# Two orders for one kernel: the task list of all engines, the places of its tiles and the engines of its PSUM copies are drawn up anew

## The chip, the cores and the metric

The kernel runs on one core of one Trainium2 chip. The core has five engines that each work through their own queue in order: TensorE (PE in the profile, with its weight loads as PEld), VectorE (DVE), ScalarE (ACT), GpSimd (POOL) and SyncE (SP). SP and POOL issue the transfers here. The metric is device time in microseconds of one launch.

## The reference

Two independent heads are computed and set side by side in the output. Head A shifts k by a filter of four taps, multiplies with v, convolves each channel over the whole sequence with a long filter (through a Fourier transform), adds a skip term and multiplies with q. Head B is a state space model: a complex projection of x, a recurrence over time with one complex factor for each state, a projection back, and a skip term.

```python
# head A, S = 2048, D = 1024
kv = k_shift * v
y_f = rfft(pad(kv)) * rfft(pad(ssm_k))
a = q * (irfft(y_f)[:S] + kv * ssm_D)
# head B, L = 2048, 1024 states
Bu = einsum("bld,pd->blp", x, B_bar)
h = Lam_bar * h + Bu[:, t, :]          # for each t
b = 2.0 * einsum("blp,dp->bld", hseq, Cmat).real + x * Dskip
return concatenate([a, b], axis=-1)
```

## The kernel before

The whole program is a list of 1489 words, the string `ORDER` (lines 68 to 188). A word such as `U.5.3.0:a22p5` names a task, its indices, and the places of new tiles: `a` is a unit of the SBUF arena (53 units of 1024 columns), `p` one of the eight PSUM banks, `h` one of three slots for the state g, `w` one of three slots for Fourier weights. A loop (lines 767 to 781) calls the tasks in the order of the list. Each engine works off its own tasks in the order of the list; between engines only data and reused places make anything wait.

Head B works in 16 chunks of 128 time steps. `x.i` loads a chunk transposed (L449, on SP). `U.i.jp.jl` is a sixteen-matmul piece of the projection on the whole 128x128 array (L468); two pieces share a bank and `ue.i.jp` copies it to SBUF on ScalarE, or `uev` on VectorE (L473). On VectorE follow `r1` and `r2` (rotation, L486 and L493), two scans `sc` (L499) and `r3`, `r4` (L486, L505); `cy` carries the last state over on ScalarE (L495). The projection back is `y` on the whole array (L515, L518) for chunks 0 to 2, 14 and 15, and `yq` for chunks 3 to 13: eight steps of 20 matmuls that use four 64x64 quarters of the array at once (L533). `ye` copies the result (L551) and `yst`, `ysp`, `ysh`, `ysg` store it.

Head A forms kv on VectorE (`kvm`, `kva`, `kvb`, `kvc`), transforms it on the whole array (`am`, L602, copied by `ae`) and stores it to HBM (`ast`). The filter goes through `hT` (whole array), `hm` (quarters, L651) and `he`. The second stage works on 16 pairs i: `lw.i` loads the weights into a slot (L666, on SP), `lh.i` and `lk.i` load rows (L671), `sh` and `sk` transform them on quarters (L682), `she` and `ske` copy the results (L691, L698), `sw` (POOL) or `swp` (SP) swap halves of one of them by a transfer (L702), `pr` multiplies on VectorE (L708), `sa` transforms back on quarters (L720), `sae` copies and `vst` stores. The last stage is `vl` (load), `a3` (whole array, L748), `a3e`, `qm` (product with q) and the store `ost` or `osp`.

At the start, `bl`, `bT`, `bc` load, transpose and copy the matrix B (whole array), and `cl`, `cT`, `cc`, `cx` the matrix C; `wb` and `wbe` spread the four filter taps over the partitions.

A name with a v at its end (`shev`, `a3ev`, `bcv`, `hdv` and so on) is the same copy on VectorE instead of ScalarE.

Of the kernel before, what the change touches and what calls it, by code (L numbers as in the profile page):

```python
# [29 lines left out]
GW = 130  # L30
# [37 lines left out]
bl.5.1:a45 bT.5.1:p6 ld_par par_T:p1 bc.5.1 bl.2.0:a25 ld_F ld_w:a26 wb.0:p0 kp.0:a0 p32 wb.2:p4 wbe.0:a8 dd wb.5:p5  # L68
bl.7.0:a32 wbe.2 bl.0.1:a34 exp1 wb.4:p3 dve2 bl.5.0:a33 dve3 bT.2.0:p6 wb.6:p2 wbe.5 bl.4.0:a49 sm_pre wbe.4
bl.4.1:a17 exp2 wb.3:p7 bl.1.1:a47 bc.2.0 wb.7:p6 wbe.3 sin0 kp.1 bT.0.1:p0 bT.7.0:p4 wbe.7 wbe.6 bl.6.1:a16 bT.4.0:p1  # L70
bc.0.1 bc.7.0 bl.0.0:a46 tabA1:a24a51a14a12 kp.-1 bT.1.1:p2 x.0:a47 par_rest cl.0.0:a39 wb.1:p7 bT.5.0:p5 sin1
bl.3.0:a31 bcv.4.0 bT.0.0:p3 wbe.1 bT.4.1:p6 bc.1.1 tabA2 kring bl.3.1:a46 kvm.3:a26 gz bT.6.1:p1 bc.0.0 bl.1.0:a23
bc.4.1 U.0.2.0:a34p4 U.0.0.0:p2 sin2 bc.6.1 bl.2.1:a22 bT.3.1:p0 bc.5.0 x.1:a33 eo kvm.2:a18 kvm.1:a40 U.0.2.1
bT.1.0:p5 kva.2 cT.0.0:p1 bT.2.1:p3 bc.2.1 bT.3.0:p6 kva.1 kvb.2:a38 kva.3 bc.3.0 U.1.2.0:a36p7 stt U.1.2.1 bl.6.0:a50
bT.6.0:p3 kvb.1:a46 bl.7.1:a32 bc.3.1 U.0.1.0:p6 bT.7.1:p0 kp.-2 bc.1.0 bc.6.0 bc.7.1 U.0.1.1 U.0.0.1 ue.0.0 ue.0.1
vp.1:a48 cl.2.0:a22 z2 z1 cl.1.1:a31 cc.0.0 x.3:a21 cl.2.1:a44 ue.1.2 ue.0.2 U.0.3.0:p3 U.0.3.1 kvb.3:a32 ue.0.3
U.1.3.0:p6 U.1.0.0:p2 kvm.0:a13 cT.2.0:p0 U.1.3.1 U.1.1.0:p5 kvc.3 kvc.2 kva.0 r1.0:a48 cc.2.0 lw.1:w0 cl.1.0:a30
ue.1.3 cx.5.1 U.1.0.1 ue.1.0 cT.1.0:p3 cc.1.0 cl.3.0:a45 kvb.0:a39 am.2.1:p4p0 ae.2.1.1:a28 rta r2.0:h0 am.2.0:p6p2
cT.2.1:p1 cc.2.1 U.1.1.1 ue.1.1 cT.3.0:p3 vp.0:a42 kvc.1 U.3.2.0:a34p7 cc.3.0 ae.2.0.1 kvc.0 ae.2.0.0 kp.3 sc.0.1
U.3.2.1 hl.0.1:a24 cl.3.1:a20 cT.3.1:p0 sc.0.0 cc.3.1 am.3.0:p5p1 ae.3.1.0:a22 ae.2.1.0 r1.1:a42 hl.0.0 U.3.3.0:p3  # L80
U.3.3.1 cT.1.1:p0 cc.1.1 kp.2 hl.1.0:a48 cl.0.1:a38 ue.3.2 am.3.1:p4p1 ae.3.1.1 U.3.0.0:p6 ue.3.3 U.3.0.1 ue.3.0
ae.3.0.0 hl.1.1 am.1.1:p0p2 ae.1.1.1:a30 cx.5.0 am.0.0:p1p7 ae.0.1.0:a18 ae.3.0.1 r3.0:a12 hdv.1 ast.2 hdv.0 ast.3
# [12 lines left out]
hm.0.1.0:p0p6 he.0.1.1.1:a38 he.0.1.0.1 y.1.0.2 vp.2:a28 hst.0.4.0 he.0.1.0.0 y.1.0.3 kvc.4 r2.2:h0 cy.2 he.0.0.0.0
ye.1.0:a18 kvc.5 am.5.1:p5p6 am.5.0:p4p2 am.4.1:p0p1 y.1.1.0:p3 y.1.1.1 he.0.1.1.0 hst.0.0.0 ae.5.1.1:a36 ae.4.0.1:a28
ae.5.1.0 hst.0.0.1 kp.5 am.4.0:p7p6 y.1.1.2 ae.4.1.0 vp.3:a26 ae.5.0.1 y.1.1.3 hl.3.0:a40 ae.5.0.0 hl.3.1 hd.3
ae.4.0.0 kvm.7:a12 hst.0.1.0 hl.2.0:a44 sc.2.1 kvc.6 hl.2.1 hd.2 am.6.0:p4p2 kva.7 ae.6.0.0:a22 ae.4.1.1 ast.5 sc.2.0
U.4.3.0:p6 ye.1.1 ae.6.1.0 kvb.7:a19 U.4.3.1 r3.2:a48 ue.4.3 am.6.1:p0p5 hT.1.1:p4 ae.6.0.1 kp.4 hc.1.1:a33 hT.1.3:p3
hc.1.3:a16 hst.0.1.1 ae.6.1.1 U.4.2.0:p2 hT.1.7:p0 U.4.2.1 yst.1 hc.1.7:a20 ue.4.2 ast.4 hT.1.6:p7 hc.1.6:a38  # L100
kvm.8:a12 U.4.0.0:p4 kvc.7 U.4.0.1 ue.4.0 r4.2 hT.1.0:p6 kva.8 ast.6 hc.1.0:a39 am.7.1:p0p2 am.7.0:p7p1 ae.7.1.0:a28
hT.1.4:p3 yst.0 hst.0.7.0 hc.1.4:a18 hst.0.2.0 ae.7.1.1 kvm.9:a48 y.2.0.0:p4 x.6:a37 ae.7.0.0 hm.1.3.1:p5p6 kvb.8:a36
he.1.3.1.1:a26 y.2.0.1 he.1.3.1.0 y.2.0.2 ae.7.0.1 cy.3 hm.1.7.1:p7p1 hm.1.3.0:p6p5 he.1.7.1.0:a16 hm.1.7.0:p3p0
he.1.3.0.1 he.1.3.0.0 he.1.7.0.1 he.1.7.0.0 kva.9 y.2.0.3 ye.2.0:a19 sc.3.1 vp.4:a22 y.2.1.0:p7 hT.1.2:p2 sc.3.0
hm.1.4.1:p0p6 hm.1.4.0:p3p5 kvc.8 hT.1.5:p4 r3.3:a44 y.2.1.1 ast.7 kvb.9:a18 y.2.1.2 hst.0.7.1 hst.1.3.1 he.1.7.1.1
y.2.1.3 he.1.4.1.0:a12 he.1.4.1.1 hst.1.3.0 hc.1.5:a20 he.1.4.0.1 he.1.4.0.0 am.8.1:p5p6 r4.3 ye.2.1 hst.1.4.1
# [84 lines left out]
def full_kernel(ctx, tc, A_q, A_k, A_v, A_shift_k, A_ssm_k, A_ssm_D, B_x, B_Lre, B_Lim, B_Bre, B_Bim,  # L191
# [645 lines left out]
```

## Time and profile before

| what | value |
|---|---|
| time, median of 3 runs | 349.76 us (347.51, 349.76, 351.59) |
| span of the profiled execution, first to last instruction | 346.5 us |
| the profiled execution's own time | not listed apart from the three |
| granted TensorE clock | 0.998 of full speed |
| TensorE busy | 328.0 us, weight loads 237.5 us |
| VectorE busy | 325.2 us |
| ScalarE busy | 272.3 us |
| GpSimd busy | 69.3 us |

Times in the profile are microseconds from the span's start. A row of groups gives line, engine, operation, tiles, count, then busy time and mean length of one in ns, then the idle time of that engine just before, with what ended it. Matmuls overlap in TensorE's pipeline and their ends are modelled, so starts are the safer reading.

### The profile page before, as it was taken

The numbers are of one execution on the slowest core, as the hardware profiler recorded it, in microseconds if no ns is written. First come the engines' busy times: TensorE is split into PE (matmuls) and PEld (weight loads), VectorE is DVE, ScalarE is ACT, GpSimd is POOL, SyncE is SP. The second block draws the span as 40 slices with busy tenths as digits, with TensorE's granted clock in tenths as the row PEclk, the third lists the DMA queues.
The fourth block names the chain that finished last, engine by engine and source line by source line (L and its number), as shares of the span: only waits on it lengthen the run. The fifth ranks groups of instructions, "written<-read, shape, count | busy, mean of one in ns | idle before, by whom it ended". The sixth has DMA issues, their size and how long they took to land.

```text
span 346.5 us, 11774 instructions
## 1 busy us (share of the span) xinstructions
PE 328.0 (95%) x5086; PEld 237.5 (69%) x5105; DVE 325.2 (94%) x263; ACT 272.3 (79%) x520; POOL 69.3 (20%) x114
## 2 busy tenths in 40 slices
PE   5889899999999999999999999999699999999994
PEld 2678789654856777688957877775376789754442
DVE  3999799999999999999999999999799999999991
ACT  6999999998999884599668899899689893314741
POOL 5000002142343163121100222211021133000021
PEclk9999999999999999999999999999999999999999
DMA  6999999979979879997896689999998898998995
GB/s 214 340 292 261 354 271 275 254 264 307 334 248 248 281 245 301 281 241 277 303 343 205 226 313 344 262 353 330 276 289 297 312 334 287 295 391 270 340 405 205
DMA packets 62752, 101.09 MB, mean 292 GB/s; under 512 B 29422, under 2 KB 31742, under 8 KB 62700
## 3 DMA queue, kind: packets, MB, share of 16 engines
q1 hardware_dynamic: 52652, 65.81, 63.7%
q0 software_dynamic: 10048, 34.52, 27.8%
q8 instruction: 40, 0.66, 0.8%
q14 instruction: 12, 0.10, 0.1%
HBM read 52.08 MB, written 33.55 MB: 247 GB/s over the span
## 4 chain that ended last, share of the span: by engine, by line
PE 68%; ACT 17%; DVE 7%; DMA 4%; issue 2%; SPq 1%; DVEq 0%; ACTq 0%
PE bank L468 24%; PE bank L533 15%; PE bank L515 10%; PE bank L682 4%; PE bank L720 4%; ACT BT L433 4%; PE bank L748 3%; PE bank L602 3%; DVE gslot L499 3%; PE bank L651 2%; ACT arena L608 2%; DMA wslot<-a_c_W 2%; ACT CT L441 2%; DVE arena L486 2%; ACT arena L473 2%
## 5 line engine op out<-in xcount | busy, mean ns | idle before, releaser
L468 PEld LDWEIGHTS <-BT 128*128 128x128 bf16 x2048 | 116.2, 98 | 13.0 <-issue 8.2
L468 PE MATMUL bank<-arena,BT 128*128 128x128 bf16 x2048 | 122.6, 219 | 1.6 <-DMA arena<-in_B_x_dram 0.9
L533 PE MATMUL bank<-CT,gslot 64*64 64x512 bf16 x1408 | 87.6, 377 | 0.0
L499 DVE TENSOR_TENSOR_SCAN gslot<-rtab,gslot 128x1040 bf16<-128x1040 f32 x32 | 73.0, 2312 | 0.1
L533 PEld LDWEIGHTS <-gslot 64*64 64x64 bf16 x1408 | 43.4, 107 | 23.9 <-ACT arena L698 0.6
L473 ACT CAST arena<-bank 128x512 bf16<-128x512 f32 x63 | 38.8, 655 | 11.6 <-PE bank L468 11.6
L608 ACT CAST arena<-bank 128x512 bf16<-128x512 f32 x64 | 37.2, 670 | 5.8 <-PE bank L602 4.9
L515 PE MATMUL bank<-CT,gslot 128*128 128x512 bf16 x154 | 38.1, 380 | 0.6 <-issue 0.3
L691 ACT CAST arena<-bank 128x512 bf16<-128x512 f32 x59 | 32.5, 615 | 7.8 <-PE bank L682 7.2
L486 DVE TENSOR_TENSOR arena<-arena,Z 128x4096 bf16<-128x4096 bf16 x16 | 36.5, 2284 | 2.2 <-ACT arena L473 2.1
L708 DVE TENSOR_TENSOR arena<-arena 128x4096 bf16<-128x4096 bf16 x16 | 36.3, 2285 | 1.7 <-ACT gslot L495 0.8
L728 ACT CAST arena<-bank 128x512 bf16<-128x512 f32 x61 | 33.3, 630 | 5.4 <-PE bank L720 5.3
L486 DVE TENSOR_TENSOR arena<-gslot,Z 128x4096 bf16<-128x4096 bf16 x16 | 36.6, 2288 | 0.3
L698 ACT CAST arena<-bank 128x512 bf16<-128x512 f32 x61 | 34.2, 616 | 3.3 <-PE bank L682 2.8
L659 ACT CAST arena<-bank 128x512 bf16<-128x512 f32 x64 | 35.2, 689 | 1.0 <-PE bank L651 0.7
L551 ACT CAST arena<-bank 128x512 bf16<-128x512 f32 x29 | 17.7, 616 | 16.3 <-PE bank L533 8.7
L582 DVE TENSOR_TENSOR arena<-arena 128x4096 bf16<-128x4096 bf16 (+3 forms) x16 | 30.0, 1886 | 0.1
L662 POOL DMA_DIRECT2D Ys_h<-arena x32 | 22.9, 728 | 29.0 <-ACT arena L659 23.1
L611 POOL DMA_DIRECT2D Ys_kv<-arena x16 | 10.9, 688 | 87.1 <-ACT arena L608 71.8
L515 PEld LDWEIGHTS <-gslot 128*128 128x128 bf16 x160 | 14.0, 98 | 17.1 <-issue 2.6
L702 POOL DMA_DIRECT2D arena<-arena x20 | 10.7, 538 | 70.8 <-ACT arena L691 46.9
L682 PE MATMUL bank<-arena,wslot 64*64 64x512 bf16 x256 | 21.5, 381 | 3.0 <-DMA wslot<-a_c_W 3.0
(104 smaller groups left out, 427.7 us busy)
## 6 DMA issues: line engine op xcount, KB each, us to landing
Ys_kv<-arena POOLq DMA_DIRECT2D x16, 512.0 KB, 4.9
Ys_h<-arena POOLq DMA_DIRECT2D x32, 256.0 KB, 3.8
arena<-Ys_h SPq DMA_DIRECT2D x16, 512.0 KB, 5.3
arena<-Ys_kv SPq DMA_DIRECT2D x16, 512.0 KB, 6.4
Vs<-arena POOLq DMA_DIRECT2D x16, 512.0 KB, 5.8
arena<-Vs SPq DMA_DIRECT2D x16, 512.0 KB, 6.9
arena<-arena POOLq DMA_DIRECT2D x20, 256.0 KB, 4.1
arena<-in_A_k_dram SPq DMA_DIRECT2D x8, 512.0 KB, 6.0
```

Source lines behind the costliest of these rows:

```text
L468: nc.tensor.matmul(pu[:, w, jl, :], BT[:, 2 * jp + jl, w, d, :], xT[:, d, :], start=(d == 0), stop=(d == ND - 1))
L473: either("ue", lambda cp, i, jp: cp(st["u", i][:, :, 2 * jp:2 * jp + 2, :], st.pop(("pu", i, jp))))
L486: nc.vector.tensor_mul(m, s_, win(Z))
L499: nc.vector.tensor_tensor_scan(gf, rtab[:].rearrange("p j t -> p (j t)"), gf, 0.0, ALU.mult, ALU.add)
L515: nc.tensor.matmul(py, h[:, w, j, 2:GW], CT[:, j, w, dh * 512:(dh + 1) * 512], start=(j == 0 and w == 0), stop=False)
L533: mm = nc.tensor.matmul(st["py", i, dh][cols, cs(r)], lhs(dh, rows, c), rhs(dh, rows), start=first, stop=last)
L608: cp(st["ysb", n2][:, p, dh * 512:(dh + 1) * 512], st.pop(("pa", n2, p, dh)))
L659: cp(o, st.pop(("pb", hf, s, e, r)).rearrange("p (n c t) -> p n c t", n=2, c=2))
L682: nc.tensor.matmul(st["ps", nm, g, l][64 * dh:64 * dh + 64, :], st["w", i][rows, a * WC:a * WC + 64], st[nm, i][rows, a, dh * 512:(dh + 1) ...
L698: cp(st["x16", i][:, a, l, :], st.pop(("ps", "k", g, l)))
L708: nc.vector.tensor_mul(hab, st.pop(("x16", i)).rearrange("p a l d -> p (a l d)").unsqueeze(1).to_broadcast([P, 2, 2 * D]), hab)
L728: cp(st["vsb", i][:, a, dh * 512:(dh + 1) * 512], st.pop(("pv", g, dh)))
```

## The change

The list is a new one with the same amount of work. Every engine's order of tasks differs, and so do nearly all places of tiles. On TensorE the same 497 tasks stand in another order; the number of whole-array and quarter tasks is unchanged. A few copies change engine. Counted by task name:

| task | before | after |
|---|---|---|
| `a3e` / `a3ev` | 25 / 7 | 28 / 4 |
| `she` / `shev` | 59 / 5 | 62 / 2 |
| `ske` / `skev` | 61 / 3 | 59 / 5 |
| `sae` / `saev` | 61 / 3 | 60 / 4 |
| `ue` / `uev` | 63 / 1 | 64 / 0 |
| `bc` / `bcv` | 15 / 1 | 14 / 2 |
| `hd` / `hdv` | 2 / 2 | 4 / 0 |
| `sw` (POOL) / `swp` (SP) | 20 / 12 | 15 / 17 |
| `ost` (POOL) / `osp` (SP) | 4 / 4 | 6 / 2 |
| `ysg` (POOL) / `ysh` (SP) | 2 / 2 | 1 / 3 |

Three tasks are also written so that more orders are possible: either half of `U` may come first, the arena places of u are taken at its first copy, and the slot of g is taken by whichever of `cy` and `r2` comes first.

```diff
 ORDER = """
...
-lh.12:a38 sw.10.1 lk.15:a6 vst.4 she.31.1 she.30.1 sw.15.0 sw.15.1 U.12.2.0:p7 sa.22:p2p4 r4.11 sk.21:p3p1 ske.21.1
-swp.10.0 ske.21.0 sa.23:p6p5 ue.12.1 U.12.2.1 U.12.0.0:p1 U.12.0.1 sae.22.1:a20 sae.23.1 sae.23.0 ue.12.2 sk.31:p0p5
...
+she.20.0 she.21.1 sc.11.0 vst.8 U.12.3.1 r3.11:a28 sh.31:p7p4 she.30.0:a2 ue.12.3:a0 U.12.1.1 she.31.0 sa.23:p2p6
+lh.12:a11 she.30.1 she.31.1 ysp.8 swp.10.0 U.12.2.1:p0 sk.20:p5p7 ue.12.1 sa.22:p3p4 yst.10 U.12.2.0 swp.10.1 lw.12:w0
...
     def U(i, jp, jl):
-        if jl == 0:
-            if ("u", i) not in st:
-                st["u", i] = sb(2).rearrange("p (w j t) -> p w j t", w=2, j=NJ)
+        if ("pu", i, jp) not in st:
             st["pu", i, jp] = bank().rearrange("p (w j t) -> p w j t", w=2, j=2)
...
-    either("ue", lambda cp, i, jp: cp(st["u", i][:, :, 2 * jp:2 * jp + 2, :], st.pop(("pu", i, jp))))
+    def ue(cp, i, jp):
+        if ("u", i) not in st:
+            st["u", i] = sb(2).rearrange("p (w j t) -> p w j t", w=2, j=NJ)
+        cp(st["u", i][:, :, 2 * jp:2 * jp + 2, :], st.pop(("pu", i, jp)))
+    either("ue", ue)
...
+    def g_(i):
+        if ("g", i) not in st:
+            st["g", i] = gslots[cur["h"].pop(0)]
+        return st["g", i]
+
     def r2(i):
-        st["g", i] = gslots[cur["h"].pop(0)]
         m = mview(i)
-        nc.vector.tensor_add(st["g", i][:, :, :, 2:GW], m[:, :, 0, :, :], m[:, :, 1, :, :])
+        nc.vector.tensor_add(g_(i)[:, :, :, 2:GW], m[:, :, 0, :, :], m[:, :, 1, :, :])
...
-    E["cy"] = lambda i: nc.scalar.copy(st["g", i][:, :, :, 1], st["g", i - 1][:, ::-1, :, GW - 1])
+    E["cy"] = lambda i: nc.scalar.copy(g_(i)[:, :, :, 1], st["g", i - 1][:, ::-1, :, GW - 1])
```

More of the change, by code (lines that the diff above doesn't have):

```diff
@@ L73 @@
[L73 to L82, printed above, removed]
@@ new lines @@
+sae.23.1:a13 sae.23.0 sk.21:p2p1 r4.11 skev.21.1:a48 U.12.0.0:p6 ske.20.0 U.12.0.1 ue.12.2 sae.22.0 ske.20.1
+yq.11.0:p0p5 ske.21.0 saev.22.1 swp.15.0 ue.12.0 sk.31:p6p7 ske.31.0:a44 pr.10 ske.31.1 sh.25:p2p3 she.25.1:a29
+r1.12:a37 yq.11.1 sh.24:p4p6 she.24.1 she.25.0 yq.11.2 yq.11.3 sk.30:p2p3 she.24.0 ske.30.0 ske.30.1 sa.21:p7p4
+sa.20:p1p6 yq.11.4 sae.21.0:a0 sw.15.1 pr.15 sk.24:p3p2 sae.20.0 yq.11.5 sae.20.1 sk.25:p7p6 lk.14:a19 yq.11.6
+ske.24.1:a48 sa.31:p1p2 vst.7 ske.24.0 sae.21.1 lh.14:a46 sae.31.0:a11 lk.13:a34 skev.25.1 ske.25.0 saev.31.1 sa.30:p3p6
@@ new lines @@
+saev.30.1 yq.11.7 sae.30.0 ye.11.1:a45 cy.12:h2 U.13.3.0:p2 lw.14:w2 swp.12.0 ye.11.0 sh.28:p3p7 lh.13:a24 lw.13:w1
+sk.28:p6p4 she.28.1:a2 sw.12.1 pr.12 sh.29:p1p5 x.15:a44 skev.28.0:a41 U.13.2.1:p0 U.13.2.0 shev.28.0 sh.27:p7p6
+she.29.0 ske.28.1 she.29.1 sk.29:p5p4 r2.12 sh.26:p3p1 she.27.1:a6 U.13.3.1 ysp.9 shev.26.0 swp.14.0 swp.14.1
+U.13.0.1:p6 ske.29.0 she.26.1 vst.10 sk.26:p1p3 she.27.0 sa.25:p5p7 sc.12.1 U.13.0.0 ske.29.1 ske.26.0:a38 sae.25.0:a49
+U.13.1.1:p5 pr.14 sw.13.0 ske.26.1 sk.27:p3p4 ue.13.0:a25 sa.24:p1p6 ue.13.2 ysp.11 sae.24.1 sae.25.1 U.15.3.1:p0
```

215 lines of the change are left out of this document (107 added, 108 removed).

## The prediction

> **What bounds the kernel now.** I read the page first, then the busy time by stage, then the chain of work that ended last, then single stretches of TensorE's timeline. The page:
>
> ```profile
> span 346.5 us, 11774 instructions
> ...
> PE 328.0 (95%) x5086; PEld 237.5 (69%) x5105; DVE 325.2 (94%) x263; ACT 272.3 (79%) x520; POOL 69.3 (20%) x114
> ...
> PE 68%; ACT 17%; DVE 7%; DMA 4%; issue 2%; SPq 1%; DVEq 0%; ACTq 0%
> ```
>
> TensorE and VectorE are both near full, and the chain runs over TensorE for 68% of the span. The busy time of six stages (columns: PE, PEld, DVE, ACT, POOL, clock, DMA share, GB/s), cut where the tasks yq.3.0, yq.5.0, yq.8.0, yq.11.0 and yq.12.0 begin on TensorE, says where each is full:
>
> ```profile
> 0.00:112.20 112.20, 102.55 (x1248) 76.38 (x1261) 104.28 (x118) 106.99 (x188) 26.36 (x47) 1.00 0.96 283
> 112.20:174.00 61.80, 61.48 (x1062) 48.69 (x1067) 61.76 (x46) 46.74 (x94) 16.65 (x25) 1.00 0.89 276
> 174.00:208.90 34.90, 34.18 (x703) 26.13 (x698) 33.98 (x20) 28.67 (x59) 4.32 (x7) 1.00 0.77 265
> 208.90:261.30 52.40, 49.30 (x956) 35.31 (x952) 48.83 (x27) 45.59 (x93) 9.04 (x15) 1.00 1.02 311
> 261.30:298.50 37.20, 37.20 (x684) 29.84 (x679) 35.71 (x26) 26.98 (x56) 8.37 (x13) 1.00 0.90 305
> 298.50:346.50 48.00, 43.30 (x461) 21.19 (x464) 40.69 (x31) 17.33 (x35) 4.56 (x7) 0.98 0.90 322
> ```
>
> In the first stage ScalarE is as full as anything (106.99 of 112.20). From 112 to 298 us TensorE idles 0.32, 0.72, 3.10 and 0.00 us, 4.1 in all. But "busy" on TensorE includes whatever an instruction spends inside the pipeline, so the question is whether it runs at its steady pace. The chain between 150 and 173 us answers it (start, length, what):
>
> ```profile
> 151.30 3.57 PE bank L468 x64
> ...
> 157.53 0.77 PE bank L682 x12
> 158.30 3.75 PE bank L468 x64
> 162.05 0.77 PE bank L682 x12
> 162.82 7.25 PE bank L468 x128
> 170.07 0.77 PE bank L682 x12
> ```
>
> L468 is the projection U, on the whole 128x128 array. Left alone, 64 of its matmuls take 3.57 us, 55.8 ns each. L682 (sh, sk) runs four 64x64 quarters of the array at once. What a quarter matmul of 512 columns costs left alone is seen where quarter work surrounds quarter work:
>
> ```profile
> 211.38 0.86 PE bank L720 x16
> ```
>
> That is 53.8 ns each. So from 157.53 to 162.05 (4.52 us) the steady price of the work is 12 x 53.8 + 64 x 55.8 ns = 4.22 us, and 0.30 us are left over. From 162.05 to 170.07 (8.02 us) it is 0.65 + 7.14 = 7.79, and 0.23 are left over. Nothing waits in either: TensorE alone is on the chain. A third stretch, from quarter work (L533) to the next quarter work:
>
> ```profile
> 135.69 0.84 PE L533 MATMUL bank<-CT,gslot 64*64 64x512 bf16 x12
> ...
> 136.39 1.04 PE L533 MATMUL bank<-CT,gslot 64*64 64x512 bf16 x16
> ...
> 137.29 1.04 PE L533 MATMUL bank<-CT,gslot 64*64 64x512 bf16 x16
> ...
> 139.40 1.07 PE L468 MATMUL bank<-arena,BT 128*128 128x128 bf16 x16
> 140.30 0.38 PE L602 MATMUL bank<-arena,F1t 128*128 128x512 bf16 x1
> 140.74 1.06 PE L468 MATMUL bank<-arena,BT 128*128 128x128 bf16 x16
> 141.63 0.59 PE L602 MATMUL bank<-arena,F1t 128*128 128x512 bf16 x2
> 142.15 0.84 PE L533 MATMUL bank<-CT,gslot 64*64 64x512 bf16 x12
> ```
>
> A yq step takes 0.90 us (136.39 to 137.29) and an am task 0.44 (140.30 to 140.74). Four yq, two U and two am are 3.60 + 1.79 + 0.88 = 6.27 us; the stretch takes 6.46, so some 0.2 us are left over again. Each time TensorE goes from quarter work to whole-array work and back it loses 0.2 to 0.3 us. That loss counts as busy and shows in no wait. From 112 us on TensorE is therefore full in earnest: its work, its switches, and 4.1 us of waits.
>
> **The change part by part.**
>
> *Order on TensorE.* The 497 TensorE tasks are the same. Call T a task on quarters (yq, hm, sh, sk, sa) and F one on the whole array (U, y, am, hT, bT, cT, wb, a3). Counted along the two lists, neighbours of different kind number 64 before and 136 after. By the six stages above: 23, 14, 4, 10, 9, 4 before; 32, 39, 11, 20, 16, 18 after. How it looks in the stretch of U.12 (bars mark the switches):
>
> ```
> before: U.12.3.0 U.12.3.1 | sk.20 sh.30 sh.31 | U.12.1.0 U.12.1.1 U.12.2.0 | sa.22 sk.21 sa.23 | U.12.2.1 U.12.0.0
> after:  U.12.3.0 U.12.1.0 | sh.30 | U.12.3.1 | sh.31 | U.12.1.1 | sa.23 | U.12.2.1 | sk.20 sa.22 | U.12.2.0 | sk.21 | U.12.0.0
> ```
>
> So 36 round trips are added. At 0.2 to 0.3 us each they cost 7 to 11 us; I take 0.26, the mean of the two samples of the chain, whose parts are the purest: **+9.4 us**. By stage: +1.2, +3.3, +0.9, +1.3, +0.9, +1.8. Nothing hides them, because TensorE has only 4.1 us of idle time in the four middle stages; VectorE and ScalarE will wait instead.
>
> [...]
>
> *Engine of the copies out of PSUM.* VectorE loses three a3e, three she and one ue copy and gains two ske and one sae: four fewer. It gains one bc copy and loses two hd additions:
>
> ```profile
> L755 DVE CAST arena<-bank 128x512 bf16<-128x512 f32 x7 | 4.8, 681 | 0.0
> L431 DVE COPY BT<-bank 128x1024 bf16<-128x1024 bf16 x1 | 0.7, 683 | 0.0
> L641 DVE TENSOR_TENSOR arena<-arena,p 128x2 bf16<-128x2 bf16 x2 | 0.2, 161 | 0.0
> L755 ACT CAST arena<-bank 128x512 bf16<-128x512 f32 x25 | 13.2, 622 | 13.8 <-remote 7.1 <-PE bank L748 6.8
> ```
>
> VectorE: -4 x 0.68 + 0.68 - 0.32 = -2.4 us. ScalarE: about 4 x 0.62 = +2.5 us, less one bc, on an engine with 74 us idle. With TensorE as the bound both are worth 0; bounds -2.4 and +2.5.
>
> *Loads and places.* lw loads one of three weight slots, so it must follow the last sa of the slot's former pair, and sh or sk waits for it. In the old list the TensorE work between these two, at steady paces, is 4.0 us for lw.13, 4.2 for lw.15, 4.4 for lw.10 and more for the rest. In the new list it is 3.8 (lw.6, lw.9), 4.0 (lw.11, lw.12, lw.15), 4.2 (lw.13), 4.4 (lw.10). What a load takes, and what happened once:
>
> ```profile
> DMA to landing us min/median/max: 2.3/4.0/7.3
> ...
> PE bank L682 <- DMA wslot<-a_c_W: 3.0, 1, 3.0
> PE bank L720 <- DVE arena L708: 0.7, 1, 0.7
> ...
> 237.65 2.04 SPq L449 DMA_TRANSPOSE arena<-in_B_x_dram  x1
> ...
> 243.68 0.34 SPq L666 DMA_DIRECT2D wslot<-a_c_W  x1
> ...
> 251.07 0.63 PE L682 MATMUL bank<-arena,wslot 64*64 64x512 bf16 x8 [3.01 <-DMA wslot<-a_c_W]
> ```
>
> The 3.0 us wait was lw.10's, issued at 243.68, two places behind the transposing load x.12 on SP. The new list puts lw.10 right behind x.12 with the same 4.4 us, so I leave that wait in. Against the median landing of 4.0 plus an issue, the six short ones may each lose some 0.3 to 0.5 us, less the switches that now stretch the work between: 0 to +2.5, and I take 0, since the 0.7 us wait for VectorE should go in exchange. Bounds of all waits together: -4.1 (all of the idle time goes) to +6 (two more like lw.10).
>
> *Queues.* Five half swaps of pr's operand move from POOL's queue to SP's:
>
> ```profile
> L702 POOL DMA_DIRECT2D arena<-arena x20 | 10.7, 538 | 70.8 <-ACT arena L691 46.9 <-PE bank L682 8.6 <-ACT arena L728 8.6
> ```
>
> At about 0.54 us of issue each, 2.7 us in all, behind which weight and row loads stand; 0 if SP has time there, +2.7 at worst. I take 0, because SP issues most loads well ahead of their readers. The last store moves from SP to POOL:
>
> ```profile
> 342.15 0.58 POOL L555 DMA_DIRECT2D out_dram<-arena  x1 [1.34 <-ACT arena L551]
> ...
> 342.76 0.34 SPq L555 DMA_DIRECT2D out_dram<-arena  x1
> ```
>
> 0.58 instead of 0.34 us to issue: +0.2, taken as 0. The three code edits (U's halves in any order, u taken at its first copy, g taken by cy or r2) issue no instruction.
>
> Sum: 346.5 + 9.4 = 355.9 us of span. The profiled execution's own time is not told apart in the list of times; its span lies 3.3 us below the median of 349.8 and 1.0 below the fastest. Added to the median: **359 us**, 2.6% slower. This case's own range, from 7 to 11 us of switches and waits between -4.1 and +4, is 353 to 365.
>
> **The rivals.**
>
> *VectorE is the pacer, and the kernel gets faster.* For it: 61.76 busy of 61.80 us from 112 to 174, and 4 copies fewer. The mechanism is that TensorE's switches fall into time in which it would have stood still for VectorE, in the stage from 112 to 174 us; it decides if the left-overs there are VectorE's pace in disguise. Then the new list is worth what it saves VectorE: 2.4 us of work, and half of the 6.0 us (0.04, 0.92, 3.57 and 1.49) that it idles in the four middle stages: 344.4 us. Against it: the chain of that stage names TensorE alone, and left-overs appear only at switches. [...] Chance 0.06.
>
> *Half of it is absorbed.* A switch costs less in small runs (0.2 us, 7.2 in sum) and all 4.1 us of idle time in the middle goes: +3.1, 352.9 us, just inside 1%. For it: the third sample. Against it: lw.10 stands where it stood. Chance 0.10.
>
> *Waits for weights multiply.* Four of the six short loads sit in the stage whose DMA share is 1.02; three more waits of 3.0 us make +18.4: 368 us. For it: three distances shrink below the shortest of before. Against it: of 13 reloaded slots only one stalled. Chance 0.14.
>
> The forecast keeps 0.70.
>
> **How the numbers follow.** The range of 351 to 367 takes the forecast's own range and reaches halfway into the two neighbours; about 0.2 is left out. A measurement of this kernel tells about 1% (3.5 us) from no change. Slower by more: the forecast and the waits, 0.84. Within 1%: the half-absorbed case, 0.10. Faster: 0.06.
>
> **What would show it.** Right: TensorE's busy time rises by 7 to 11 us with the same 5105 weight loads; short runs of L682 or L720 between short runs of L468, each round trip 0.2 to 0.3 us over the steady price; yq.5.0 begins about 4.5 us later than 173.8, with VectorE's idle share up in that stage. Wrong: VectorE still full from 112 to 174 and TensorE's tasks on their old pace; or a gain in span with 136 switches in the trace. If the span grows but by L682 waits on wslot, the third rival holds.

## The result, and the profile after

| kernel | median us | lowest to highest | ratio to before, 95% interval |
|---|---|---|---|
| before (4 runs beside it) | 350.66 | 347.51 to 351.59 | 1 |
| after (4 runs) | 372.47 | 368.31 to 374.69 | 1.0545 [1.0426, 1.0664] |

The new order is slower by 21.8 us in the medians and by 19.1 by the ratio (5.45% of 350), where 9.4 were forecast. Ratios leave disturbed executions out and medians do not; where the two differ below, the ratio counts. The profiled execution of after is its longest, 374.69 us with a span of 372.9, so what is read from that profile is more than the typical loss.

The page of after, with the lines that answer to those of before:

```profile
span 372.9 us, 11773 instructions
...
PE 340.6 (91%) x5080; PEld 233.2 (63%) x5105; DVE 325.3 (87%) x258; ACT 276.5 (74%) x527; POOL 68.7 (18%) x110
...
PE 22%; DMA 5%; DVE 2%; issue 1%; ACT 0%; POOL 0%; ACTq 0%; DVEq 0%
```

TensorE is busy for 340.6 us instead of 328.0, as a price of switches would make it (some 4 of these 12.6 us are lost at half clock, as shown below), but it also idles 32.3 us instead of 18.5. The same six stages by busy time (columns as before):

```profile
0.00:120.80 120.80, 105.89 (x1238) 80.45 (x1255) 107.23 (x118) 107.64 (x189) 25.56 (x45) 0.99 0.93 262
120.80:185.70 64.90, 64.24 (x1059) 48.37 (x1062) 62.66 (x47) 47.43 (x95) 17.14 (x25) 1.00 0.89 264
185.70:231.10 45.40, 38.18 (x716) 21.84 (x708) 35.20 (x19) 29.93 (x61) 5.71 (x9) 0.92 0.86 233
231.10:281.90 50.80, 49.48 (x945) 32.72 (x944) 45.42 (x27) 44.61 (x91) 8.06 (x13) 1.00 0.94 303
281.90:314.40 32.50, 31.82 (x573) 22.62 (x574) 29.78 (x20) 25.73 (x51) 6.20 (x9) 1.00 0.91 274
314.40:372.90 58.50, 51.01 (x572) 27.22 (x576) 45.00 (x32) 21.20 (x42) 6.03 (x9) 0.99 0.86 298
```

The stage that begins at yq.5.0 stands out: TensorE idles 7.2 of 45.4 us, and the granted clock is 0.92. The stage before it, 61.8 us long in the old list, takes 64.9; the prediction gave it 3.3 more. The waits name it (us in all, times, longest):

```profile
DVE arena L714 <- DMA arena<-arena: 15.0, 4, 9.2
...
PE bank L726 <- DVE arena L714: 6.0, 1, 6.0
...
PE bank L608 <- ACT arena L474: 4.8, 1, 4.8
...
ACT arena L645 <- DMA arena<-in_A_ssm_k_dram: 4.6, 1, 4.6
...
PE bank L416 <- DMA arena<-in_B_B_im_dram: 4.2, 2, 3.6
```

L714 is pr, L726 sa, L608 am, L474 ue, L645 hd, L416 the transposes at the start. The timeline shows how the longest comes about (idle time ahead of an instruction in brackets):

```profile
176.19 1.47 SPq L677 DMA_DIRECT2D arena<-Ys_kv  x3
179.07 0.87 SPq L677 DMA_DIRECT2D arena<-Ys_h  x2
179.99 2.15 SPq L448 DMA_TRANSPOSE arena<-in_B_x_dram  x1
...
180.90 1.63 POOL L708 DMA_DIRECT2D arena<-arena  x3 [7.10 <-ACT arena L697]
...
197.66 4.49 DVE L714 TENSOR_TENSOR arena<-arena 128x4096 bf16<-128x4096 bf16 x2 [9.23 <-DMA arena<-arena]
...
192.01 0.84 PE L539 MATMUL bank<-CT,gslot 64*64 64x512 bf16 x12
...
200.01 1.07 PE L726 MATMUL bank<-arena,wslot 64*64 64x512 bf16 x8 [6.02 <-DVE arena L714]
200.86 1.49 PE L539 MATMUL bank<-CT,gslot 64*64 64x512 bf16 x12
```

SP issues five row loads of 512 KB and then, from 179.99 to 182.14, the transposing load x.11. In the middle of that POOL issues three swaps. They land 16 us later, within 1.3 us of each other; pr.0 waits 9.2 us for one of them, sa.1 waits 6.0 us for pr.0. After that wait twelve yq matmuls take 1.49 us, not 0.84: the clock is halved (0.50 granted until 204.9). The swaps' landing times over the whole kernel, and the clock of that stretch:

```profile
DMA to landing us min/median/max: 2.8/4.6/16.4
```

```profile
196.00:206.00 10.00, 5.99 (x80) 2.78 (x84) 8.34 (x4) 2.15 (x4) 0.40 (x1) 0.66 0.61 213
```

The switches are there too. The rows of a quiet stretch:

```profile
167.87 0.41 PE L688 MATMUL bank<-arena,wslot 64*64 64x512 bf16 x4
168.21 1.07 PE L465 MATMUL bank<-arena,BT 128*128 128x128 bf16 x16
169.20 0.41 PE L688 MATMUL bank<-arena,wslot 64*64 64x512 bf16 x4
169.55 1.96 PE L465 MATMUL bank<-arena,BT 128*128 128x128 bf16 x32
171.44 0.41 PE L688 MATMUL bank<-arena,wslot 64*64 64x512 bf16 x4
```

From 167.87 to 169.20 are 1.33 us for 4 x 53.8 + 16 x 55.8 ns = 1.11: 0.22 left over. From 169.20 to 171.44 it is 0.24.

The account of the profiled spans, 346.5 to 372.9, by left-over time (a stretch less its tasks at steady paces, as in the prediction), cut at the first and the last quarter task on TensorE:

| part | before | after | difference |
|---|---|---|---|
| first matmul | 3.5 | 3.9 | +0.4 |
| up to the first quarter task | 12.6 | 19.5 | +6.9 |
| middle: round trips at 0.235 each (31; 67) | 7.3 | 15.7 | +8.5 |
| middle: the stretch with sa.1 (173.6 to 199.7; 185.5 to 218.4), less its one round trip | 1.1 | 10.1 | +9.0 |
| middle: all else | 5.1 | 4.2 | -0.9 |
| after the last quarter task | 5.3 | 7.9 | +2.6 |

### The profile page after: what moved, and what is told of

It reads as the page before. It is cut to its first block, busy times and chain, and to the rows that moved or that the text cites. A ratio compares the mean times of both kernels' runs of the same rounds, so it can differ in the third digit from the quotient of the medians.

```text
span 372.9 us, 11773 instructions
## 1 busy us (share of the span) xinstructions
PE 340.6 (91%) x5080; PEld 233.2 (63%) x5105; DVE 325.3 (87%) x258; ACT 276.5 (74%) x527; POOL 68.7 (18%) x110
## 5 line engine op out<-in xcount | busy, mean ns | idle before, releaser
L465 PE MATMUL bank<-arena,BT 128*128 128x128 bf16 x2048 | 127.7, 220 | 0.4 <-DVE BT L430 0.3
L539 PE MATMUL bank<-CT,gslot 64*64 64x512 bf16 x1408 | 91.2, 383 | 1.8 <-DVE gslot L511 1.3
L539 PEld LDWEIGHTS <-gslot 64*64 64x64 bf16 x1408 | 37.8, 108 | 34.6 <-issue 5.8
L474 ACT CAST arena<-bank 128x512 bf16<-128x512 f32 x64 | 37.9, 609 | 19.7 <-PE bank L465 19.4
L714 DVE TENSOR_TENSOR arena<-arena 128x4096 bf16<-128x4096 bf16 x16 | 36.4, 2284 | 16.9 <-DMA arena<-arena 15.0
L734 ACT CAST arena<-bank 128x512 bf16<-128x512 f32 x60 | 32.9, 611 | 17.3 <-PE bank L726 16.8
L614 ACT CAST arena<-bank 128x512 bf16<-128x512 f32 x64 | 34.9, 612 | 8.1 <-PE bank L608 7.6
L697 ACT CAST arena<-bank 128x512 bf16<-128x512 f32 x62 | 33.9, 615 | 6.1 <-PE bank L688 4.6
L665 ACT CAST arena<-bank 128x512 bf16<-128x512 f32 x64 | 35.0, 622 | 4.5 <-PE bank L657 3.8
L704 ACT CAST arena<-bank 128x512 bf16<-128x512 f32 x59 | 33.3, 624 | 4.0 <-PE bank L688 2.8
L761 ACT CAST arena<-bank 128x512 bf16<-128x512 f32 x28 | 15.2, 597 | 15.2 <-PE bank L754 9.8
L521 PEld LDWEIGHTS <-gslot 128*128 128x128 bf16 x160 | 13.8, 98 | 17.3 <-issue 3.9
L726 PE MATMUL bank<-arena,wslot 64*64 64x512 bf16 x256 | 19.0, 394 | 6.0 <-DVE arena L714 6.0
L688 PE MATMUL bank<-arena,wslot 64*64 64x512 bf16 x256 | 23.4, 387 | 0.7 <-DMA wslot<-a_c_W 0.7
```

Source lines behind the costliest of these rows:

```text
L465: nc.tensor.matmul(pu[:, w, jl, :], BT[:, 2 * jp + jl, w, d, :], xT[:, d, :], start=(d == 0), stop=(d == ND - 1))
L474: cp(st["u", i][:, :, 2 * jp:2 * jp + 2, :], st.pop(("pu", i, jp)))
L521: nc.tensor.matmul(py, h[:, w, j, 2:GW], CT[:, j, w, dh * 512:(dh + 1) * 512], start=(j == 0 and w == 0), stop=False)
L539: mm = nc.tensor.matmul(st["py", i, dh][cols, cs(r)], lhs(dh, rows, c), rhs(dh, rows), start=first, stop=last)
L614: cp(st["ysb", n2][:, p, dh * 512:(dh + 1) * 512], st.pop(("pa", n2, p, dh)))
L665: cp(o, st.pop(("pb", hf, s, e, r)).rearrange("p (n c t) -> p n c t", n=2, c=2))
```

## The experiments

Variants whose name begins with "before" start from the old list, the others from the new.

### The transposing load x.11 moved: x11_late, x11_early, x2_late, x2_x11_late

```diff
-... lk.1:a7 lk.0:a24 ... lh.2:a34 x.11:a33 ... sw.3.1 ... lh.4:a21 ... lk.4:a42 ...
+... lh.2:a34 ... sw.3.1 ... lh.4:a21 ... lk.4:a42 x.11:a33 ...  (x11_late)
+... x.11:a33 lk.1:a7 lk.0:a24 ... lh.2:a34 ... sw.3.1 ...       (x11_early)
-... hl.0.1 U.3.1.0:p4 x.2:a52 ... lw.3:w2
+... hl.0.1 U.3.1.0:p4 ... lw.3:w2 x.2:a52                       (x2_late; x2_x11_late has both)
```

> The new list with one word moved: the transposing load x.11 stands behind the row load lk.4 instead of ahead of lh.4, so that the swaps sw.3.0, sw.0.1 and sw.3.1 are issued before it. Theory (a transposing load behind a full queue holds every transfer issued near it for 16 to 17 us): the three swaps land within 7 us of their issue, VectorE's wait of 9.2 us at pr.0 and TensorE's of 6.0 us at sa.1 are gone, TensorE's half clock after it too, and the time falls by 9 to 11 us against the new list, to 361 to 364 us. Rival (the swaps are slow because five row loads of 512 KB are ahead of them, whatever x.11 does): they still take over 12 us and the time stays within 3 us of 372. Second rival (the wait goes but VectorE's or ScalarE's pace behind it takes the time back): no wait at sa.1, time 368 or more.

> The new list with one word moved the other way: x.11 stands ahead of lk.1, the first of the five row loads, while SP has nothing else to issue. Theory: x.11 is issued near 171 us into a short queue and lands within 8 us; row loads and swaps behind it land within 8 us of issue; pr.0 waits under 2 us; time 361 to 364 us. Rival (row loads ahead of the swaps are the cause): the same five row loads and the same swaps collide, pr.0 still waits over 6 us, time 369 or more.

> The new list with the transposing load x.2 moved behind lw.3, four words of SP's queue later, so that hl.0.0, hl.1.1, hl.1.0, hl.0.1 and cl.0.1 go ahead of it. Theory: hl.0.1 lands within 8 us of its issue (13.0 before), hd.0 on ScalarE waits under 1 us (4.6 before), ue.3.0 is copied in time and TensorE's wait of 4.8 us at am.0.1 with the half clock behind it is gone: the time falls by 5 to 7 us, to 365 to 367 us. Rival (four loads of 512 KB land that late by their size alone): hl.0.1 still takes over 11 us and the time stays within 2 us of 372.

> Both moves, x.2 behind lw.3 and x.11 behind lk.4, in the new list. Theory (the two held groups of transfers are all that the prediction lacked, and the 36 added changes between quarter and whole-array work cost the rest): both waits are gone and the time is the old list's plus 8 to 11 us, 358 to 361 us; TensorE loses 0.23 to 0.26 us in each round trip. Rival (the new list has slack against each single hold, so the two gains overlap or are lost to VectorE): 364 us or more.

| kernel | median us (lowest to highest) | ratio, 95% interval |
|---|---|---|
| x11_late | 363.03 (361.55 to 365.77) | 1.0372 [1.0290, 1.0453] |
| x11_early | 364.23 (360.73 to 365.57) | 1.0381 [1.0294, 1.0469] |
| x2_late | 369.05 (364.37 to 370.81) | 1.0462 [1.0334, 1.0591] |
| x2_x11_late | 362.68 (362.02 to 363.93) | 1.0357 [1.0292, 1.0422] |

One word of 1489, moved either way, takes 8 to 9 us off the median and about 6 us by the ratios (1.0545 to 1.0372 and 1.0381). The swaps of x11_late:

```profile
DMA to landing us min/median/max: 2.9/3.9/7.0
```

and its timeline where sa.1 had waited until the clock fell; TensorE now works through at full pace (12 yq matmuls in 0.82 us):

```profile
198.22 0.60 PE L727 MATMUL bank<-arena,wslot 64*64 64x512 bf16 x8
198.65 0.82 PE L540 MATMUL bank<-CT,gslot 64*64 64x512 bf16 x12
```

The share of x.11 in the profiled execution is thus the wait of 6.0, 1.2 more at 190.9 (for which the profile names no releaser; gone in x11_late), and half of the 4.9 us after 200.0 that ran at half clock (2.4): 9.6 us. That execution is the longest of four; by the ratios x.11 is worth 6.1 us of the 19.1, roughly, since the intervals of after and x11_late just overlap. The hold is not peculiar to one execution: in x2_late, where x.11 stands as in after, the three swaps took 13.2 to 14.3 us, sa.1 waited 5.0 us, and 6.8 us at half clock came with it again.

The theory on x.2 failed. The four times that hl took (minimum, median, maximum of its landings) in after, in x11_late where x.2 was not moved, and in x2_late where it was:

```profile
DMA to landing us min/median/max: 5.3/11.0/13.0
```

```profile
DMA to landing us min/median/max: 5.2/6.9/10.3
```

```profile
DMA to landing us min/median/max: 5.1/7.0/10.1
```

The 4.8 us wait at am.0.1 is 1.8 in x11_late and 1.7 in x2_late: most of it belonged to that one execution, and x.2's place has no part in the rest. Both moves together give no more than x.11 alone.

### What holds the transfers: x11_swaps_sp, before_xzT, before_xzP, before_xzT2

x11_swaps_sp leaves x.11 in its place behind the five loads, but the three swaps come from SP, behind it in the same queue.

```diff
-... sw.3.0 ... sw.0.1 ... x.11:a33 sw.3.1 ...
+... x.11:a33 swp.3.0 swp.0.1 swp.3.1 ...
```

> The new list with x.11 where it stands, but with the three swaps sw.3.0, sw.0.1 and sw.3.1 taken from POOL's queue and issued on SP right behind x.11. The depth of the queue ahead of x.11 is the same; what goes is a second queue whose transfers are issued while x.11's are waiting. Theory Q (the hold comes from two queues interleaving with a transposing load): x.11 lands within 10 us, the swaps within 10 us of their issue, pr.0 waits under 4 us, time 362 to 366 us. Theory D (a transposing load behind five row loads holds what comes after it, from whichever queue): x.11 and the swaps again take over 14 us and the time stays at 369 to 375 us.

364.04 us (360.90 to 366.93), 1.0354 [1.0257, 1.0451]. The queue, and the landings of all swaps:

```profile
178.47 0.87 SPq L678 DMA_DIRECT2D arena<-Ys_h  x2
179.39 1.71 SPq L449 DMA_TRANSPOSE arena<-in_B_x_dram  x1
181.21 1.84 SPq L709 DMA_DIRECT2D arena<-arena  x3
```

```profile
DMA to landing us min/median/max: 2.4/4.2/7.3
```

Same depth, same transfers, but one queue: x.11 lands 8.2 us after its issue (16.8 in after), no swap takes over 7.3, and the ratio is that of x11_late. Theory D falls.

Is such a load enough by itself? An extra one, read by nobody, in the old list; before_xzP loads the same 256 KB untransposed.

```diff
+    def xz(i):
+        t_ = sb(1).rearrange("p (d t) -> p d t", d=ND)
+        nc.sync.dma_start_transpose(t_, x[i * T:(i + 1) * T, :])   # before_xzP: an ordinary load
-... lh.2:a32 sw.1.1 ... swp.0.0 ...
+... lh.2:a32 xz.11:a19 sw.1.1 ... swp.0.0 ...                       (before_xzT, before_xzP)
+... lh.2:a32 sw.1.1 ... swp.0.0 xz.11:a19 ...                       (before_xzT2)
```

> The old list with one extra transposing load of chunk 11 (256 KB, into unit 19, which is free there; nobody reads it) set on SP behind the row loads lh.8, lk.3 and lh.2, just ahead of the swaps that POOL issues near 169 us. Theory Q (a transposing load that waits in a filled queue while POOL issues holds all that is in flight): POOL's swaps sw.0.1, sw.1.0 and sw.3.1 land 12 us or more after their issue (7.6 before), pr.1 on VectorE starts 4 us or more later, and the kernel is slower by 4 to 10 us: 354 to 360 us. Rival (256 KB more to move, 1 us): 349 to 351 us.

> The control: the same extra 256 KB at the same place as an ordinary load, not transposed. Theory Q: the swaps land within 9 us and the time stays at 349 to 351.5 us. If it is slower by as much as the transposing one, the queue's load decides and not the transposition.

> The extra transposing load in the old list again, now behind swp.0.0, so that SP is still issuing it (near 169.3 to 171 us) when POOL issues sw.1.0 and sw.3.1; in the first try POOL's issues came 0.8 us after its end. Theory Q2 (transfers are held when POOL issues them while SP is in the middle of issuing a transposing load into a filled queue; over all traces so far 23 of 29 POOL transfers that took over 9 us were such): sw.1.0 and sw.3.1 land 11 us or more after their issue (7.6 in the old list), pr.1 starts 3 us or more later, the time is 353 to 358 us. Rival (being issued together is not enough): they land within 9 us, 349 to 351.5 us.

before_xzT: 354.10 us (350.38 to 359.39) beside 352.59 for before, 1.0055 [0.9999, 1.0112]: nothing held. before_xzP: 353.08 (347.16 to 355.81), no ratio. before_xzT2: 351.70 (351.08 to 355.06), 1.0119 [1.0047, 1.0191]. The swaps' landings in the three, in that order:

```profile
DMA to landing us min/median/max: 2.2/4.8/8.6
```

```profile
DMA to landing us min/median/max: 2.2/4.4/7.6
```

```profile
DMA to landing us min/median/max: 2.2/4.4/12.1
```

The difference between the first and the third is when POOL issues. In before_xzT it begins 0.8 us after SP has done with the transposing load. In before_xzT2 it falls into it:

```profile
170.30 2.17 SPq L454 DMA_TRANSPOSE arena<-in_B_x_dram  x1
...
169.97 1.59 POOL L707 DMA_DIRECT2D arena<-arena  x3 [7.71 <-ACT arena L696]
```

There the third swap took 12.1 us and the second 8.1, so one of the two that were expected to be held was. pr.1 was not late; pr.3 stood still for 2.1 us behind pr.0, TensorE waited 2.0 us for it, and the clock was then halved for 3.4 us. The time missed the expected 353 to 358 us. Over the twenty profiles (before, after, the eighteen variants) POOL issued 265 transfers between 0.8 us before the start and the end of a transposing issue on SP: 25 of them took over 9 us to land, 16.4 at most, median 5.8. Of the other 1690 (median 4.6) 8 did, 9.5 at most. For POOL's transfers in these profiles, being issued together thus comes close to a necessary condition for a long hold and is far from sufficient. What else it needs is open.

### What a switch costs: before_tinyT and before_tinyF

One tiny matmul (64 columns) in the middle of 36 U tasks of the old list, on a quarter or on the whole array; the next matmul overwrites its result.

```diff
         for w in range(2):
             for d in range(ND):
+                if w == 1 and d == 0 and jl == 0 and 3 <= i <= 11:
+                    nc.tensor.matmul(pu[0:64, 1, 0, 0:64], BT[0:64, 2 * jp, 1, 0, 0:64], xT[0:64, 0, 0:64], start=True, stop=True)
```

> The old list as it is, with one tiny quarter matmul (64x64 of the array, 64 columns, into a place of the bank that the next matmul overwrites) set into the middle of 36 U tasks, the first half of each pair of chunks 3 to 11. The order on every engine stays; TensorE goes 36 times from whole-array to quarter work and back inside a run of whole-array work. Theory (the change of kind itself costs 0.23 to 0.26 us a round trip, and nothing absorbs it): 8 to 10 us more, 358 to 361 us. Rival (VectorE sets the pace from 112 us on): 350 to 352 us. Rival (half absorbed by waits): near 354.5 us.

> The control: the same 36 places, the same 64 columns, but on the whole 128x128 array, so without a change of kind. Theory: 36 x 0.03 to 0.06 us, 1 to 2 us more at most, 350 to 352 us. If it is slower by 6 us or more, an added matmul costs by itself and not by its tiling.

before_tinyT: 356.02 us (355.23 to 356.19), 1.0177 [1.0113, 1.0241]. before_tinyF: 351.54 (347.44 to 355.43), 1.0034 [0.9977, 1.0090]. The quarter one first, then the whole-array one, each with the U matmuls around it:

```profile
127.88 1.96 PE L470 MATMUL bank<-arena,BT 128*128 128x128 bf16 x32
129.77 0.21 PE L469 MATMUL bank<-arena,BT 64*64 64x64 bf16 x1
129.92 0.62 PE L470 MATMUL bank<-arena,BT 128*128 128x128 bf16 x8
```

```profile
126.88 1.95 PE L470 MATMUL bank<-arena,BT 128*128 128x128 bf16 x32
128.67 0.19 PE L469 MATMUL bank<-arena,BT 128*128 128x64 bf16 x1
128.70 0.61 PE L470 MATMUL bank<-arena,BT 128*128 128x128 bf16 x8
```

2.04 against 1.82 us: the change of kind alone is 0.22 us a round trip, so 36 are 8.0 us of TensorE's time. The end moved by 4.5 us (medians) to 5.0 (ratios). Part of the rest was taken from waits: the left-over beyond round trips and tiny matmuls in the middle part is 4.5 us with the quarter ones, 6.6 with the whole-array ones. So the expectation was right in the price and too high in what reaches the end.

### TensorE's order changed alone: before_118, before_perm64, x11_late_94

Only TensorE's queue is rearranged, each task by a few places (at most 6, 9 and 10), chosen so that by the profile's times no operand would be late and no copy delayed by more than 0.6 us (1.0 in x11_late_94).

```diff
 before_118:     64 -> 118 neighbours of different kind
 before_perm64:  64 -> 64, as many tasks moved
 x11_late_94:   136 -> 94, from x11_late
```

> The old list with TensorE's tasks alone set in another order (the other engines' orders and all places stay): neighbours of different kind number 118 instead of 64, so 27 round trips between quarter and whole-array work are added, each task moved by a few places at most. Theory (each round trip costs 0.23 to 0.26 us and nothing absorbs it): 27 x 0.235 = 6.3 us more, 355 to 359 us. Rival (VectorE sets the pace and the switches fall into time in which TensorE would stand still): 349 to 352 us. Rival (half absorbed): near 353.5 us.

> The control to the 118: the old list with about as many TensorE tasks moved by as many places, but with 64 neighbours of different kind as before. If only the number of switches matters, 349 to 352 us, as before. If moving tasks costs by itself (copies come later, banks come free later), it is slower by 3 us or more.

> The new list with x.11 behind lk.4, and TensorE's tasks regrouped so that 94 instead of 136 neighbours differ in kind; other engines and places as they were. Theory: 21 round trips fewer, 21 x 0.235 = 4.9 us less than the 363.0 us of x.11 moved alone: 356.5 to 359.5 us. Rival (the rest of the new list's loss is waits, and TensorE only waits longer): 361 us or more.

366.68 us (364.94 to 367.80), 1.0476 [1.0412, 1.0541]; 363.09 (362.69 to 364.57), 1.0386 [1.0325, 1.0446]; 382.85 (380.30 to 383.58), 1.0930 [1.0859, 1.1001]. The theory failed in all three, and the control, in which its second case came true, shows why: moving tasks by a few places costs 13 us with no switch added. Its waits on TensorE are many and short:

```profile
PE bank L683 <- DMA wslot<-a_c_W: 2.6, 1, 2.6
PE bank L534 <- ACT arena L699: 1.9, 4, 0.7
PE bank L683 <- ACT arena L729: 1.4, 2, 0.8
```

A reading of it that no run tested: ScalarE still copies in its old order, so one late sk holds every copy behind it, and each copy that is late frees a bank late. The longest waits of L534 are yq steps at their half (yq.5.4, yq.7.4), which by the code wait for the copy of a task set between them and the step before. In the middle part the left-over is 31.9 us with 118 and 25.0 with 64: 6.9 us for 27 round trips, 0.25 each, while the times differ by only 3.6. Regrouping the new list made it 19.8 us slower, so by the price of 0.235 its 21 round trips saved 4.9 us and the regrouping lost some 25 us.

### The rest of the new list: x11_late_yo14, x11_late_bl, x11_late_bl_ast2

```diff
-ye.14.0:a40
+ye.14.0:a2                                              (x11_late_yo14)
-... bl.2.0:a38 bl.7.0:a40 ... bl.1.0:a14 ... bl.3.1:a21 ...
+... bl.2.0:a38 bl.3.1:a21 bl.7.0:a40 ... bl.1.0:a14 ...   (x11_late_bl)
-... ast.2 ast.0 ... ast.1 ast.3 ...
+... ast.0 ... ast.1 ast.2 ast.3 ...                       (x11_late_bl_ast2, with the one above)
```

> The new list with x.11 behind lk.4 and the result tile of chunk 14 at a unit that has been free for long (2 instead of 45, which the store ost.0 still reads). Theory (TensorE's wait of 1.8 us near the end comes from this place: ye.14.0 stands still on ScalarE until ost.0 has landed): ye.14.0 starts within 0.5 us of y.14.0.3's end, the wait at a3 goes, and 1.5 to 2 us are saved against x.11 moved alone: 361 to 362 us. Rival (the end is set by the last stores): within 0.5 us of 363.0.

> The new list with x.11 behind lk.4 and, at the start, the load bl.3.1 moved from behind bl.1.0 to ahead of bl.7.0, in the order in which TensorE transposes them. Theory (TensorE's wait of 3.6 to 4.6 us near 19 us, and the half clock of 3.4 to 6.8 us that follows it, are most of the 3 us that the start still loses): the wait is cut into several under 2 us each, no half clock before 60 us, and 2 to 4 us are saved against 363.0: 359 to 361 us. Rival (the start is bound by what all loads together take, the order does not matter): 362 to 364 us.

> As the one before, and POOL's store ast.2 moved behind ast.0 and ast.1, so that POOL issues nothing while x.2 and the loads hl wait. Theory Q: hl.0.1 lands within 8.5 us of its issue (9.5 to 13.0 before), TensorE's wait at am.0.1 (1.3 to 4.8 us) is under 0.7 us, 1 to 2 us less than the one before. Rival (2 MB of loads ahead take that long): hl.0.1 still takes 9.5 us or more and the time is the same within 0.7 us.

x11_late_yo14: 362.34 us (362.20 to 364.03), 1.0367 [1.0309, 1.0425], 0.7 us less than x11_late in the median and 0.2 by the ratio, which is within the noise. (The place left is unit 40 in this list; the 45 of the expectation is that of the old one.) The wait at a3 stayed as long, for another releaser (before it: 1.80 <-ACT arena L558):

```profile
345.96 0.61 PE L755 MATMUL bank<-arena,Gt 128*128 128x512 bf16 x2 [1.81 <-DMA arena<-Vs]
```

Two things were late at once, and the profile names the later one.

x11_late_bl: 365.30 us (363.27 to 368.11), 1.0411 [1.0292, 1.0530]; not faster. The wait of 4.4 us was cut up as expected, but the same stretch then met another hold: ast.2, issued 1.5 us into the issue of x.2, took 11.6 us, and TensorE waited 2.2 us for cl.0.1 near 61 us. The start itself gained nothing either: its waits still add up to 4.8 us (2.0, 0.9 and 1.9), and TensorE ran at half pace for longer. Rows of the transposes in before, x11_late and x11_late_bl, in that order:

```profile
14.93 1.51 PE L417 MATMUL bank<-ident,arena 128*128 128x128 bf16 x24 [0.62 <-DMA arena<-in_B_B_re_dram]
```

```profile
19.68 4.45 PE L417 MATMUL bank<-ident,arena 128*128 128x128 bf16 x40 [4.37 <-DMA arena<-in_B_B_im_dram]
```

```profile
27.32 1.06 PE L417 MATMUL bank<-ident,arena 128*128 128x128 bf16 x8
```

Their starts are 56 ns apart in the first and 107 ns in the other two. The pace of 56 ns is there for good from 13.8 us on in before, 24.0 in after, 24.8 in x11_late and 30.8 in x11_late_bl. The clock column of the stage tables does not show this.

x11_late_bl_ast2: 367.16 us (361.74 to 367.58), 1.0377 [1.0149, 1.0604]; unclear. hl.0.1 landed in 9.0 us (8.5 expected) and the wait at am.0.1 was under 0.5, but ast.3 and a store of hst, issued with x.4, now took 12.1 and 11.3 us. Moving POOL's stores away from one transposing load put them beside the next.

### The old list's own hold: before_x12, before_vsp

```diff
-... lw.11:w1 ... vst.8 ... x.12:a52 ... vst.6 ... lw.10:w2 ... swp.11.0 ...
+... x.12:a37 lw.11:w1 ... vst.8 ... vst.6 ... lw.10:w2 ... (before_x12; ye.9 and ye.13 change places)
+... lw.11:w1 ... x.12:a52 ... lw.10:w2 ... swp.11.0 vsp.8 vsp.6 ... (before_vsp: both stores on SP)
```

> The old list with the transposing load x.12 issued ahead of lw.11, before POOL's stores vst.8 and vst.6 are issued, at another free place (ye.9 and ye.13 take other free places in exchange); nothing else moves. Theory (a transposing load that waits while another queue issues holds what stands near it): lw.10 lands within 4.5 us (7.3 before), TensorE's wait of 3.0 us for its weight slot goes, and the time falls by 2 to 3.5 us, ratio 0.990 to 0.995, 346.5 to 348.5 us. Rival (lw.10 is late because of its queue's load alone): ratio 0.998 to 1.002.

> The old list with POOL's two stores vst.8 and vst.6, which are issued while SP issues the transposing load x.12, given to SP behind swp.11.0, after x.12 has landed; x.12 and lw.10 stay where they are. Theory Q2: x.12 lands within 7 us (11.0 before), lw.10 within 4.5 us (7.3 before), TensorE's wait of 3.0 us for it goes and 1.5 to 3 us are saved, ratio 0.991 to 0.996. Rival (the wait moves to the next weight load, as it did when x.12 itself was moved): ratio 0.998 to 1.003.

before_x12: 353.40 us (345.63 to 360.38), 0.9953 [0.9885, 1.0022]. before_vsp: 350.83 (347.12 to 355.54), 1.0023 [0.9977, 1.0069]. In before_vsp x.12 lands in 5.0 us (11.0 in before) and lw.10 in 2.3 (7.3), as expected. But the wait for a weight slot is only handed on, to lw.15 here (the row) and, in three waits that add up to 3.0 us again, to other slots in before_x12:

```profile
256.19 1.07 PE L682 MATMUL bank<-arena,wslot 64*64 64x512 bf16 x8 [2.70 <-DMA wslot<-a_c_W]
```

In before_x12 the load was issued beside two other transfers of POOL's, which landed in 6.4 and 6.8 us. In before_vsp the two stores of 512 KB were put ahead of lw.15 on SP, so this wait is of the experiment's own making. Neither variant is faster than before.

## Why the prediction was right in direction and wrong in size

**What bounds the kernel** was read rightly: TensorE, with a loss at each change between quarter and whole-array work that shows in no wait. The tiny matmuls show it with nothing else changed, 0.22 us a round trip. "From 112 us on TensorE is therefore full in earnest" holds to 298.5 us only: in the prediction's own table it idles 4.7 us in the last stage and 9.7 in the first, and 3.0 of the 9.4 us were counted there. The direction was not luck: with x.11 out of the way the new list is still 3.7% slower.

**The switches' term** (+9.4 us, bounds 7 to 11) held as TensorE time: 8.0 to 8.5 us for 36 round trips, at 0.22 to 0.24 instead of 0.26. That "nothing hides them" was too strong: in the old list 4.5 to 5.0 of 8.0 us reached the end. That drew on the few waits that were there, as the rival of half absorption had it. Of the prediction's signs, busy time rose by 12.6 us and not by 7 to 11, some 4 of them being lost at half clock, and yq.5.0 began 11.9 us later and not 4.5.

**The term that failed is that of the waits**: "The six short ones may each lose some ... I take 0", with "bounds of all waits together: -4.1 ... to +6", and "Queues ... I take 0, because SP issues most loads well ahead of their readers." In the profiled execution they cost some 17.6 us (the rows of the account other than the round trips and the first matmul). The range was drawn with +4 in place of the +6; neither reaches that far. The bounds were drawn from one kind of wait, the weight slots, because the old list had one such. The weight slots were harmless: 0.7 us in all on sh and sk (busy time, mean ns, idle before and its releaser):

```profile
L688 PE MATMUL bank<-arena,wslot 64*64 64x512 bf16 x256 | 23.4, 387 | 0.7 <-DMA wslot<-a_c_W 0.7
```

and lw.10's wait of 3.0 us, which was to stay, went. So the third rival, "waits for weights multiply", came nearest in time (368) by a mechanism that did not occur. The missed mechanism was in the quoted rows: x.12 at 237.65 on SP, and behind it lw.10, which took 7.3 us to land. It was read as lw.10's bad luck in the queue, not as what a transposing load can do to transfers issued beside it; one of POOL's stores took 11.4 us there. The question that would have found x.11 is where the new list issues POOL transfers during a transposing load; its order of words alone cannot tell that to the microsecond, but "x.11" stands between sw.0.1 and sw.3.1 there.

**Swaps on other queues** were costed by their issue time (0 to 2.7 us). Three of those left on POOL cost 6.1 us by the ratios, and 9.6 in the profiled execution, by when they were issued.

**Clock**: taken as constant. With the waits of 4.8 and 6.0 us on TensorE came 3.4 and 6.8 us at half clock, 1.7 and 2.4 us more: in the profile of after the granted clock is 0.50 from 58.1 to 61.5 us (the first wait ended at 57.4) and from 198.0 to 204.9 us (the second began 2.0 us before its wait ended). What sets the length of such a stretch was not tested.

**Copies and store**: taken as 0 and unseen in any wait. VectorE's busy time did not fall (325.2 and 325.3 us), so the 2.4 us that the copies were to take off it are not to be found.

**Still open**: x11_late remains 13 us above before by the ratio (12 in the medians). By its profile, the 13.3 us of span above that of before (359.8 against 346.5) divide into 8.5 for switches, 3.2 and 0.4 at the start, 2.9 at the end, and 1.7 gained on waits in the middle. At the start TensorE runs at half pace until 24.8 us instead of 13.8: the forty transposes shown above lose 40 x 51 ns = 2.0 us by it. What makes the pace rise when it does was not tested, and the end's cause was not found.

## What to carry to other kernels

In a schedule that fills every engine, an order is judged by its waits: look at a new one first by where transfers of different queues meet (here three swaps beside one transposing load took 16.0 to 16.4 us to land, which cost 6.1 us by the ratios), then by the sum of the work. A price that shows in no wait (here the change of tiling, 0.22 us a round trip) is measured by adding it alone with a control of equal work, not by permuting the order, because here the permutation cost 13 us where 6 were to be measured. The two waits of after that came with a halved clock cost some 35 to 40% more than their length.

## What the runs showed of the hardware that was not expected

- With a transposing load (x.11) issued on SP behind 2.5 MB of loads and POOL issuing meanwhile, x.11 took 16.8 us to land, POOL's swaps 16.0 to 16.4 and SP's next load 16.7; with the swaps issued on SP, x.11 took 8.2 us and the swaps at most 7.3. Over twenty profiles 25 of 265 POOL transfers issued so took over 9 us, against 8 of 1690 others.
- The hold is not the same in each execution: hl's longest landing was 13.0 us in after and 9.5 to 11.3 in five variants whose list has the same loads there (x11_early, x11_late, x11_late_94, x11_late_yo14, x11_swaps_sp).
- The length of a wait alone does not say whether the clock is halved: lw.10's 3.0 us in before left it at full, 2.0 us in before_xzT2 came with 3.4 us at half clock.
- TensorE came to full pace for good at 13.2 to 21.5 us in the ten profiles of the old list and its variants, at 22.4 to 30.8 in the ten of the new one; until then, but for one stretch of 3.4 to 6.9 us in some, 128-column matmuls start 107 ns apart instead of 56.
- A single 64x64 matmul between whole-array matmuls costs 0.22 us more than a 128x128 one of the same 64 columns.
